# A block's layer norms: means, variances and shifts computed on GpSimd instead of VectorE

## The chip, the core and the metric

The kernel runs on one core of a Trainium2 chip. A core has five engines with queues of their own, each in order: TensorE (PE in the profile, its weight loads are PEld), VectorE (DVE), ScalarE (ACT), GpSimd (POOL) and SyncE (SP, which here only starts DMAs). They wait for one another through semaphores. The metric is the time of one execution in device microseconds (us); lower is better. The profile is one execution on the chip, taken with the hardware profiler; its span, from first to last instruction, is somewhat shorter than the time that the runs give.

## The reference, cut to what matters

`x` has 2048 rows of 512 bfloat16 values. Three layer norms, a windowed attention (32 heads, 8 keys each, two rows apart) and an MLP that mixes the rows:

```
def _layernorm(x, axis=-1, eps=1e-05):
    m = jnp.mean(x, axis=axis, keepdims=True)
    v = jnp.var(x, axis=axis, keepdims=True)
    return (x - m) / jnp.sqrt(v + eps)
...
    h = _layernorm(x, axis=-1) * (1 + ca) + sa          # first norm
    x = x + ga * _A_ref(h, A_wqkv, A_wo)                # attention
    h = _layernorm(x, axis=-1) * (1 + cb) + sb          # second norm
    x = x + gb * _B_ref(h, B_w1, B_b1, B_w2, B_b2)      # MLP over rows
    return x
...
    def _B_ref(x, w1, b1, w2, b2):
        h = _layernorm(x, axis=-1)                      # third norm
        u = _gelu(jnp.einsum('bsd,sf->bdf', h, w1) + b1)
        y = jnp.einsum('bdf,fs->bds', u, w2) + b2
        return y.transpose(0, 2, 1)
```

The six modulation rows (`sa` to `gb`) come from a small matrix product of `silu(c)`.

## The kernel before, in words

The 2048 rows are 16 tiles of 128 rows, in five chunks of 2, 4, 4, 4 and 2 tiles. A chunk goes through: statistics of the first norm (`ln1s`), reciprocal standard deviation (`rstd1`), normalized tiles (`n1`), their transposes (`tr` on TensorE with evictions `hT`, or DMA transposes `xt` in the last three chunks), the projections (`qkv`, evicted by `ev`), products of queries with shifted keys on VectorE (`qk`, 128x4096 elements for a chunk of four tiles), their reduction on TensorE (`red`), maximum, exponential and reciprocal (`max`, `sub`, `exp`, `esum`, `rcp`, `smB`), products of weights with shifted values on VectorE (`pv`), reduction on TensorE (`pvacc`, evicted by `oev`), the output projection (`wo`, evicted by `x1` with the sum of each row), the sum of squares (`ln2q`), the second norm (`rstd2`, `n2`, then `aff`, which multiplies and adds the modulation rows), the statistics of the third norm (`ln3s`) and its result (`rstd3`, `h3`). The MLP's first product (`mlp1`) sums over rows, so it takes one tile of `h3` after another; partial sums are parked in SBUF (`park`) and added later (`inj`, `padd`). After GELU the second product (`mlp2`) and the output (`fin`, `st_out`) follow.

The order of all this is written out by hand: `ORDER` is one list of names, and each engine issues its own in just that order. So an instruction that waits holds back everything behind it on its engine, whatever is ready. `add` records an operation with engine and dependencies; a helper issues them all, so the profile has one source line (L133), and its groups are told apart by their tiles. The tiles to know: `st` (statistics of BN_STATS, 6 values a row), `mv` (mean and variance), `lv` (logarithm), `rs` (reciprocal standard deviation), `nb` (shift, minus mean times `rs`), `sums` (sum and sum of squares), `big` (the attention products), `lsb` (softmax weights), `h` (normalized tiles), `junk` (the unused output of squaring).

The layer norms before:

- `ln_stats`: on VectorE, BN_STATS and an aggregation to `mv`, tile by tile. For tiles 10 to 13 of the first norm ScalarE sums and squares instead, and VectorE forms the variance (`ln1v`).
- The second norm takes sum and square from ScalarE, except tiles 14 and 15; VectorE forms the variance of a group of tiles in two instructions (`ln2m`).
- `ln_rstd`: ScalarE takes a logarithm and an exponential for a group (the chunk in the first norm; 2, 2, 4 or 1 tiles in the others). VectorE multiplies out the shift (`nb`), unless the whole group is normalized on VectorE.
- `ln_norm`: one instruction per tile, on ScalarE, GpSimd or VectorE as the letters A, P and D in `NE` say.

There are 25 such groups: 5 of the first norm, 10 of the second and 10 of the third. `NBIG` gives four buffers for the attention products; `psS` are six PSUM tiles, which the evictions free.

Of the kernel before, what the change touches and what calls it, by code (L numbers as in the profile page):

```python
# [13 lines left out]
P = 128  # L14
# [168 lines left out]
consts ld_x_1_2 act_table ld_x0 ld_x_1_4 ld_c ld_x_2_8 ld_x1 ident ld_x_2_6 ld_wmod1 ln1s3 halo0 ld_wqkv1 cps  # L183
ln1s2 warm2 ld_wqkv0 silu_exp ld_wmod0 ln1s0 ln1s4 ln1s1 ln1s5 rstd1_0 ld_x_4_14 nb1_0 ln1s9 rstd1_1 n1_0 n1_1
silu_dve nb1_1 ld_wqkv2 ln1s8 fill:2:70 tr0_0 n1_2 n1_4 modcols1 ln1s7 hT0_3:a n1_5 n1_3 ld_x_3_10 hT0_2:d a1col
hT0_0:a fill:4:16 tr1_2 wsc1_2:d ld_b1 hT0_1:a wsc1_3:d wsc1_0:a tr1_0 wsc1_1:d ln1s6 hT1_2:a ld_wmod2 qkv0_10
ld_x_3_12 wsc0_0:d rstd1_2 wsc0_1:d qkv0_12 wsc0_2:d hT1_1:a nb1_2 n1_8 n1_9 wsc0_3:d modcols0 hT1_0:d ld_wmod3
hT1_3:a qkv0_00 sab ev0_12:d n1_6 ld_wmod4 qvb0 ln1s14 ld_wo1 qkv0_02 qvb_cp0 ln1s15 ev0_00:a wsc2_2 qvb1
wsc2_0:d qkv1_00 wsc2_3 ev0_10:a ev0_02:d ln1s10 wsc2_1:d qkv1_10 qvb_cp1 qk0_0 ev1_10:a qkv0_22 qk0_1 n1_7
qkv0_20 ln1s13 qk0_2 qkv1_02 xt6 red0_0 ev1_00:a qk0_3 red0_1 red0_2 ev0_22:a ld_wmod5 qkv1_22 qk1_0 ev0_20:a  # L190
qkv1_12 ev1_02:a vd0_1 red0_3 ev1_12:a mask qkv1_11 vd0_0 ln1s11 max0 xt8 qk1_2 qkv1_01 ev1_11:a sub0 qkv1_03
ev1_01:a xt9 exp0 qkv1_13 qk1_1 ev1_03:a xt7 esum0 ev1_13:a qkv1_20 rcp0 vd0_2 ln1s12 qkv1_21 smB0 qk1_3 a2_0_3
modcol2 rstd1_4 qkv1_23 a2_0_0 ev1_22:a a2_0_2 halo_v1:a red1_0 ev1_20:a a2_0_1 red1_1 ln1v10 ln1v12 ln1v11
ln1v13 nb1_4 red1_2 rstd1_3 n1_15 ld_wo3 red1_3 nb1_3 ld_wo2 mcols0 n1_11 n1_10 qkv2_00 max1 ev1_21:a n1_14 xt10
qkv2_02 ev2_00:a pv0_0 qkv2_10 n1_12 ld_wo0 pv0_1 qkv2_11 vd0_3 ev2_10:a ev2_02:a qkv2_12 qk2_0 n1_13 qkv2_01
xt12 ev2_12:a pvacc0_0 ev2_01:a sub1 qk2_2 xt13 qkv2_03 exp1 qkv2_13 xt11 ev2_11:a ev2_03:a qkv2_22 qk2_1
ev2_13:a esum1 ev1_23:a qkv2_21 rcp1 vd1_2 red2_0 smB1 ev2_21:a ld_b2 red2_1 qk2_3 halo_v2:a a2_1_1 red2_2
pvacc0_1 a2_1_3 qkv3_00 a2_1_2 qkv3_10 a2_1_0 pv0_2 mrowt0 vd1_1 qkv2_20 ev3_10:a pv0_3 ev3_00:a red2_3 mrows0:a
qkv2_23 ev2_20:a st_row0 max2 halo_k3:p ev2_22:a vd1_3 qkv3_11 qk3_0 xt14 qkv3_22 ev3_11:a pvacc0_2 ld_row0
pvacc0_3 sub2:q oev0_2:a vd1_0 pv1_2 qkv3_02:q exp2 qkv3_12 ev3_02:a ev2_23:a qkv3_01 pv1_3 oev0_0:a vd2_2 esum2  # L200
modcol3 xt15 rcp2 ev3_12:a woq_s qkv3_20 ev3_01:a pvacc1_3 smB2 ev3_20:a red3_0 qk3_1 ev3_22:a a2_2_0 pvacc1_2
wo1 a2_2_1 vd2_3 qkv3_13:q x1_1 a2_2_2 pv1_1 vd2_1 wo0 ev3_13:a a2_2_3 qkv4_02 ld_w1_0_512 oev1_2:a mcols1 pv1_0
ld_w1_0_0 oev1_3:a mrowt1 qkv3_03 mrows1:a x1_0 st_row1 qkv4_00 ev3_03:a vd2_0 ln2q1 qk3_2 pvacc1_0 ev4_02:a
red3_1 pvacc1_1 oev1_0:a qkv3_23:q oev1_1:a qk3_3 ev4_00:a wo3:q ln2q0 wo5:q pv2_2 qkv4_22:q x1_5 ev3_23:a wo2:q
ld_row1 ln2q5 ld_w1_0_896 ln2m0 halo_v3:a wo4:q x1_3 pv2_1 x1_2 red3_2 x1_4 red3_3 ln2q3 qkv3_21:q pv2_3 rstd2_0
qkv4_20 ln2q2 ev3_21:a ev4_22:a vd3_3 pvacc2_1 nb2_0 max3 pvacc2_2 n2_0 warm0 ln2q4 vd3_0 n2_1 ln2m2 sub3 pv2_0
pvacc2_3 oev2_2:a exp3 rstd2_2 esum3 oev2_1:a aff0 pvacc2_0 rcp3 oev2_0:a qkv4_10 oev2_3:a ln2m4 nb2_2 smB3
warm3 n2_2 ev4_10:a ln3s0 wo6 a2_3_0 n2_3 ln3s1 a2_3_1 rstd2_4 wo7 x1_6 vd3_1 aff2 rstd3_0 a2_3_2 biascols wo9:q
ev4_20:a a2_3_3 nb2_4 nb3_0 ln3s3 n2_5 n2_4 vd3_2 warm1 ln3s2 h3_1 h3_0 qkv4_12 aff4 rstd3_2 wo8 x1_7 ld_w2_0
nb3_2 ln3s5 h3_3 h3_2 ln2q6 ln3s4 mlp1_0_6_0 ev4_12:a pv3_0 mlp1_0_3_0 x1_9 rstd3_4 mlp1_0_5_0 x1_8 mlp1_0_0_0  # L210
biascols_cp:a ln2q8 nb3_4 pv3_1 halo_v4:a mlp1_0_2_0 h3_4 vd4_1 h3_5 mlp1_0_1_0 ln2q9 pv3_2 ld_w2_1 mlp1_0_2_4
vd4_2 ln2q7 mlp1_0_0_4 vd4_0 mlp1_0_3_4 park0_0:a mlp1_0_1_4 mlp1_0_5_4:q park0_1:a ln2m6 vd4_3 pv3_3 park0_2:a
pvacc3_0 pvacc3_1 oev3_0:a ld_w1_0_1152 pvacc3_2 oev3_1:a mlp1_0_4_0:q rstd2_6 oev3_2:a qk4_2 pvacc3_3 park0_3:a
mlp1_0_7_0 oev3_3:a nb2_6 qk4_1 n2_6 mlp1_0_6_4 mlp1_0_4_4 n2_8 qk4_0 wo12:q ld_w1_0_1408 n2_7 n2_9 qk4_3 wo10:q
park0_4:a aff6 x1_12 red4_0 wo13:q ld_w2_3 park0_5:a ln2q12 red4_1 red4_2 x1_10 red4_3 wo11:q max4 ln2q10 ln3s9
x1_13 sub4:q mlp1_0_8_0:q exp4 ln3s8 ln2q13 mlp1_0_11_0 esum4 ln3s7 rcp4 mlp1_0_12_0 park0_6:a ln3s6 x1_11
mlp1_0_10_0 smB4 rstd3_6 ln2m12 a2_4_2 mlp1_0_9_0 h3_7 rstd2_12 h3_6 a2_4_3 ln2q11 h3_9 mlp1_0_8_4 ln2m13 a2_4_0
nb2_12 ln2m11 n2_12 mlp1_0_7_4 a2_4_1 ln2m10 h3_8 rstd2_10 ld_w2_4 aff12 mlp1_0_9_4 rstd2_13 rstd2_11 nb2_10
ln3s12 mlp1_0_9_8 mlp1_0_7_8 n2_10 mlp1_0_8_8 nb2_13 pv4_0 park0_7:a mlp1_0_12_4 ld_w1_0_1664 park0_8:a
mlp1_0_11_4 nb2_11 pv4_2 n2_13 mlp1_0_10_4 rstd3_12 pv4_1 park0_9:a mlp1_0_12_8 n2_11 mlp1_0_10_8 pv4_3 inj1_4  # L220
mlp1_0_11_8 ld_w1_1_0 park0_10:a pvacc4_2 ld_w1_1_640 park0_11:a pvacc4_0 nb3_12 aff11 pvacc4_1 h3_12 pvacc4_3
mlp1_0_13_0 aff10 oev4_0:a oev4_2:a aff13 mlp1_0_13_4 ln3s10 wo15 ld_w2_5 ln3s13 rstd3_10 mlp1_0_13_8 wo14 x1_15
rstd3_13 park0_12:a inj1_0 nb3_13 ln2s15 mlp1_1_0_6 nb3_10 x1_14 rstd2_15 mlp1_1_4_6 park0_13:a nb2_15 ln2s14
n2_15 inj1_3 inj1_6 ld_w1_1_896 inj1_5 mlp1_1_6_6 rstd2_14 aff15 h3_10 mlp1_1_3_6 ln3s15 mlp1_1_6_10 ln3s11
mlp1_1_0_10 rstd3_15 inj1_1 mlp1_1_1_6 park1_0:a nb3_15 h3_15 n2_14 rstd3_11 aff14 mlp1_1_5_6 h3_13 ln3s14
mlp1_1_5_10 mlp1_1_1_10 inj1_2 ld_w1_2_0 mlp1_1_2_6 h3_11 rstd3_14 park1_1:a h3_14 mlp1_1_4_10 mlp1_1_3_10
mlp1_1_2_10 mlp1_1_9_10 park1_2:a ld_w1_1_1408 park1_3:d mlp1_1_7_10 padd1_9 park1_4:a park1_5:d mlp1_1_8_10
padd1_7 gelu7 mlp1_1_10_10 park1_6:a mlp1_2_2_11 ld_w1_2_640 padd1_10 mlp1_2_2_14 mlp1_2_0_11 padd2_2
mlp1_2_0_14 ld_w2_7 gelu2 mlp1_2_1_11 padd2_0 mlp1_2_1_14 gelu0 mlp1_1_12_10 padd2_1 gelu10 padd1_8 gelu1
# [12 lines left out]
def kernel(  # L242
# [52 lines left out]
    def T(shape, dtype, name):  # L295
        return sb.tile(shape, dtype, name=name)
# [38 lines left out]
    epscol = T([P, 1], F32, "epscol")  # L335
# [17 lines left out]
    for l in range(3):  # L353
        for nm, n in (("st6", 6), ("mv", 2), ("lv", 1), ("rs", 1), ("nb", 1)):
            ln_t[nm, l] = T([P, NST, n], F32, f"{nm}_{l}")
# [14 lines left out]
    def ln_stats(l, st, src, reads, name):  # L370
        st6, mv = ln_t["st6", l], ln_t["mv", l]
        if l == 0 and st in LN1A:
            def fa():
                nc.scalar.activation(junk[:], src, ACT.Identity, scale=1.0 / D, accum_out=mv[:, st, 0:1])
                nc.scalar.activation(junk[:], src, ACT.Square, scale=D ** -0.5, accum_out=st6[:, st, 0:1])
            add("act", 1.36, fa, reads=reads + ["act_table"], writes=[("sq", l, st)], name=name)
            add("dve", 0.15, lambda: nc.vector.scalar_tensor_tensor(
                mv[:, st, 1:2], mv[:, st, 0:1], mv[:, st, 0:1], st6[:, st, 0:1], op0=ALU.mult, op1=ALU.subtract,
                reverse1=True), reads=[("sq", l, st)], writes=[("mv", l, st)], name="ln1v" + name[4:])
            return  # L380

        def fd():
            nc.vector.bn_stats(st6[:, st, :], src)
            nc.vector.bn_aggr(mv[:, st, :], st6[:, st, :])
        return add("dve", 0.86, fd, reads=reads, writes=[("mv", l, st)], name=name)

    def ln_rstd(l, g0, n, name, var=None, vreads=None):
        mv, lv, rs, nb = (ln_t[k, l] for k in ("mv", "lv", "rs", "nb"))
        sl = slice(g0, g0 + n)
        var = mv[:, sl, 1] if var is None else var  # L390

        def fa():
            nc.scalar.activation(lv[:, sl, 0], var, ACT.Ln, bias=epscol[:, 0:1])
            nc.scalar.activation(rs[:, sl, 0], lv[:, sl, 0], ACT.Exp, scale=-0.5)
        reads = [("mv", l, st) for st in range(g0, g0 + n)] if vreads is None else vreads
        add("act", 0.54, fa, reads=reads + ["ident", "act_table"], writes=[("rs", l, g0)], name="rstd" + name)
        if vreads is None and NE[l][g0:g0 + n] == "D" * n:
            return
# [640 lines left out]
```

## Time and profile before

| what | value |
|---|---|
| time, median of 2 runs | 207.16 us (206.71 to 207.61) |
| span of the profiled execution | 204.6 us, 4223 instructions |
| VectorE, products of query and key, 128x4096 | 12 x 2284 ns |
| VectorE, products of weight and value, 128x4096 | 12 x 2286 ns |
| VectorE, BN_STATS | 30 x 677 ns |
| VectorE, aggregation of one tile | 30 x 182 ns |
| VectorE, shifts | 21, 145 to 159 ns each |
| ScalarE, logarithm / exponential of a group | 25 x 291 ns / 25 x 204 ns |
| GpSimd, normalization of one tile | 11, 813 ns (9 of `xx`) and 774 ns (2 of `h`) on average |
| granted TensorE clock | full in all windows but the last |

Busy time in us of each window of 5 us, from answers of the trace:

| window | PE | DVE | ACT | POOL |
|---|---|---|---|---|
| 0 to 5 | 1.91 | 1.32 | 1.46 | 2.32 |
| 10 to 15 | 4.74 | 4.77 | 4.73 | 1.52 |
| 45 to 50 | 5.00 | 5.00 | 2.04 | 0.53 |
| 75 to 80 | 4.26 | 4.90 | 4.97 | 0.77 |
| 90 to 95 | 4.32 | 4.91 | 4.69 | 0.77 |
| 110 to 115 | 4.49 | 4.83 | 4.00 | 0.00 |
| 140 to 145 | 5.00 | 2.11 | 2.11 | 0.00 |

Busy shares say how long an engine had an instruction under way. A row of the timeline reads: start, duration, engine, line, operation, output and inputs, sizes, count, and in brackets the idle time of the engine before it with what ended it. "x2" is two instructions merged, with their joint duration. A row of the view of waits names who waited, for whom, the sum, how often, and the longest. Neighbouring instructions of one engine overlap by some hundredths of a microsecond in the records.

### The profile page before, as it was taken

How to read it: one execution, taken by the hardware profiler on the slowest of the kernel's cores; microseconds unless marked ns; L12 is line 12 of the kernel's file. 1: busy time of each engine (PE TensorE's matmuls, PEld its weight loads, DVE VectorE, ACT ScalarE, POOL GpSimd, SP SyncE). 2: the span in 40 equal slices, each digit the busy share in tenths (PEclk: the TensorE clock that was granted, in tenths of full speed). 3: DMA queues.
4: the chain of work that ended last, by engine and by line, in shares of the span. 5: the costliest groups of instructions: out<-in, count | busy, mean ns of one | idle time of the engine just before them, and what ended most of it. 6: DMA issues, size and time to landing. Idle time of an engine off the chain costs nothing.

```text
span 204.6 us, 4223 instructions
## 1 busy us (share of the span) xinstructions
PE 194.7 (95%) x1655; PEld 103.5 (51%) x1655; DVE 163.3 (80%) x260; ACT 120.6 (59%) x283; POOL 13.0 (6%) x36
## 2 busy tenths in 40 slices
PE   3999999999999997989899999999999999999994
PEld 3988554454455553554344445444444444444453
DVE  2899999999999999999999999975473204369365
ACT  2398998994666899989898876683762000000000
POOL 4122001100000001240000000100000000000000
PEclk9999999999999999999999999999999999999999
DMA  5999494646958976194975179946990930121121
GB/s 141 330 380 348 117 239 107 161 98 201 247 186 267 308 234 251 25 272 110 289 200 115 26 157 263 288 131 200 340 304 3 232 88 16 39 77 51 51 82 51
DMA packets 55111, 35.93 MB, mean 176 GB/s; under 512 B 24628, under 2 KB 52404, under 8 KB 55092
## 3 DMA queue, kind: packets, MB, share of 16 engines
q1 hardware_dynamic: 55084, 35.67, 61.4%
q8 instruction: 13, 0.21, 0.4%
q14 instruction: 6, 0.05, 0.1%
q10 hardware_dynamic: 8, 0.00, 0.0%
HBM read 22.55 MB, written 2.10 MB: 121 GB/s over the span
## 4 chain that ended last, share of the span: by engine, by line
PE 65%; DVE 20%; issue 5%; DMA 5%; SPq 3%; ACT 2%; DVEq 0%
PE psS L133 62%; DVE big L133 9%; DVE h L133 3%; PE psL L133 3%; SPq L133 3%; DVE st L133 3%; DMA wst<-in_B_w_dram 2%; DMA xx<-in_A_x_dram 2%; ACT h L133 1%; DVE mv L133 1%; DVE m L133 1%; DVE lsb L133 1%; DVE ls L133 0%; DVE nb L133 0%; DVE woq L133 0%
## 5 line engine op out<-in xcount | busy, mean ns | idle before, releaser
L133 PE MATMUL psS<-h,wst 128*128 128x512 bf16 (+1 forms) x254 | 50.7, 379 | 1.2 <-POOL h L133 0.7
L133 PE MATMUL psS<-hT,w_qkv 128*128 128x512 bf16 (+3 forms) x312 | 46.2, 339 | 0.3 <-ACT w_qkv L133 0.3
L133 PEld LDWEIGHTS <-wst 128*128 128x128 bf16 (+1 forms) x356 | 28.7, 98 | 32.2 <-issue 3.2
L133 PEld LDWEIGHTS <-w_qkv 128*128 128x128 bf16 (+1 forms) x354 | 29.5, 111 | 21.3 <-issue 3.2
L133 DVE TENSOR_TENSOR big<-a2sb,vD 128x4096 bf16<-128x4096 bf16 (+1 forms) x20 | 36.9, 1876 | 0.0
L133 DVE TENSOR_TENSOR big<-q_sb,k_f 128x4096 bf16<-128x4096 bf16 (+1 forms) x20 | 36.3, 1857 | 0.0
L133 DVE SCALAR_TENSOR_TENSOR h<-psS,bcol,rows_bc 128x512 f32<-128x512 f32 (+2 forms) x18 | 12.4, 690 | 24.4 <-PE psS L133 24.2
L133 PE MATMUL psS<-gT,big 128*128 128x512 bf16 x112 | 24.8, 379 | 0.0
L133 PEld LDWEIGHTS <-big 128*128 128x128 bf16 x144 | 12.0, 97 | 13.2
L133 PEld LDWEIGHTS <-ident 128*128 128x128 bf16 (+1 forms) x203 | 13.9, 111 | 5.9 <-issue 2.8
L133 PE MATMUL psS<-woq,o_sb 128*32 128x512 bf16 (+1 forms) x172 | 16.6, 380 | 0.0
L133 ACT ACTIVATE h<-xx,nb,rs 128x512 bf16<-128x512 bf16 x19 | 15.0, 807 | 0.8 <-DVE nb L133 0.7
L133 DVE TENSOR_TENSOR psS<-psS,gT 128x512 f32<-128x512 f32 x14 | 9.3, 696 | 7.0 <-PE psS L133 7.0
L133 ACT ACTIVATE junk<-xx 128x512 bf16<-128x512 bf16 x22 | 13.8, 626 | 0.2
L133 POOL TENSOR_SCALAR h<-xx,rs,nb 128x512 bf16<-128x512 bf16 x9 | 7.3, 813 | 101.3 <-DVE nb L133 84.0
L133 ACT ACTIVATE lv<-mv,epscol 128x1 f32<-128x1 f32 (+2 forms) x25 | 7.3, 291 | 9.3 <-DVE mv L133 8.4
L133 DVE BATCH_NORM_STATS2 st<-xx 128x6 f32<-128x512 bf16 x14 | 9.5, 678 | 4.0 <-DMA xx<-in_A_x_dram 4.0
L133 ACT ACTIVATE gT<-psS,bcol 128x512 bf16<-128x512 f32 x14 | 8.7, 688 | 6.4 <-DVE psS L133 6.4
L133 PEld LDWEIGHTS <-group 128*32 128x32 bf16 x288 | 6.8, 96 | 10.2 <-issue 4.8
L133 DVE TENSOR_TENSOR h<-h,rows_bc 128x512 bf16<-128x512 bf16 (+2 forms) x20 | 11.5, 581 | 0.5
L133 DVE TENSOR_TENSOR h<-h,xx 128x512 bf16<-128x512 f32 (+2 forms) x18 | 11.4, 633 | 0.6
L133 ACT ACTIVATE gT<-psS 128x512 bf16<-128x512 f32 x19 | 10.8, 587 | 1.6 <-PE psS L133 1.5
(94 smaller groups left out, 220.4 us busy)
## 6 DMA issues: line engine op xcount, KB each, us to landing
vD<-v_sb SPq DMA_DIRECT2D x12, 524.5 KB, 3.8
big<-in_B_w_dram SPq DMA_DIRECT2D x4, 896.0 KB, 8.2
vD<-v_sb SPq DMA_DIRECT2D x8, 268.5 KB, 3.0
wst<-in_B_w_dram SPq DMA_DIRECT2D x3, 640.0 KB, 5.3
out_dram<-h SPq DMA_DIRECT2D x15, 128.0 KB, 1.8
xx<-in_A_x_dram SPq DMA_DIRECT2D x7, 256.0 KB, 6.1
wst<-in_B_w_dram SPq DMA_DIRECT2D x2, 800.0 KB, 4.8
gT<-in_w_mod_dram SPq DMA_DIRECT2D x3, 512.0 KB, 6.1
```

The lines of the kernel that those rows point to most:

```text
L133: r = fn(*a, **k)
```

## The change

What VectorE and ScalarE deliver stays: BN_STATS, sums and squares. All that follows on one to eight values a row moves to GpSimd, for the whole group at once. `lnm` is a new operation of GpSimd: for statistics of BN_STATS six instructions (half-row means subtracted, both halves added, the difference squared, the sum of the variances scaled with the epsilon added, the two added, the mean scaled into the shift), for sums four. ScalarE's logarithm reads its result (with a factor of 0.25 for BN_STATS), and the shift `nb` is one more instruction of GpSimd after the exponential. Aggregations, `ln1v` and `ln2m` are gone. All normalizations now read `rs` and `nb`. A memset (`epscol`) goes too, since the epsilon is now an immediate. In `ORDER`, each `lnm` stands immediately ahead of its `rstd`, and four `nb` are new (for groups that had none); the rest is as it was.

```diff
     def ln_stats(l, st, src, reads, name):
...
-        def fd():
-            nc.vector.bn_stats(st6[:, st, :], src)
-            nc.vector.bn_aggr(mv[:, st, :], st6[:, st, :])
-        return add("dve", 0.86, fd, reads=reads, writes=[("mv", l, st)], name=name)
+                nc.scalar.activation(junk[:], src, ACT.Identity, scale=1.0 / D, accum_out=sums[:, st, 0:1])
+                nc.scalar.activation(junk[:], src, ACT.Square, scale=D ** -0.5, accum_out=sums[:, st, 1:2])
+            return add("act", 1.46, fa, reads=reads + ["act_table"], writes=[("st", l, st), ("sums", st)], name=name)
+        return add("dve", 0.66, lambda: nc.vector.bn_stats(st6[:, st, :], src), reads=reads, writes=[("st", l, st)],
+                   name=name)
+
+    def ln_rstd(l, g0, n, name, kind):
+        st6, sm, mv, rs, nb = (ln_t[k, l] for k in ("st6", "sm", "mv", "rs", "nb"))
         sl = slice(g0, g0 + n)
-        var = mv[:, sl, 1] if var is None else var
+        g = nc.gpsimd
+
+        def f():
+            if kind == "bn":
+                g.tensor_tensor(mv[:, sl, 0], st6[:, sl, 1], st6[:, sl, 4], op=ALU.subtract)
+                g.tensor_tensor(sm[:, sl, :], st6[:, sl, 1:3], st6[:, sl, 4:6], op=ALU.add)
+                g.tensor_tensor(mv[:, sl, 0], mv[:, sl, 0], mv[:, sl, 0], op=ALU.mult)
+                g.tensor_scalar(mv[:, sl, 1], sm[:, sl, 1], 4.0 / D, 4.0 * EPS, op0=ALU.mult, op1=ALU.add)
+                first, neg = sm[:, sl, 0], -0.5
+            else:
+                neg = -1.0 if l == 0 else -1.0 / D
+                first = sums[:, sl, 0]
+                g.tensor_tensor(mv[:, sl, 0], first, first, op=ALU.mult)
+                g.tensor_scalar(mv[:, sl, 0], mv[:, sl, 0], -neg * neg, EPS, op0=ALU.mult, op1=ALU.add)
+            second = mv[:, sl, 1] if kind == "bn" else sums[:, sl, 1]
+            g.tensor_tensor(mv[:, sl, 0], mv[:, sl, 0], second, op=ALU.add)
+            g.tensor_scalar(nb[:, sl, 0], first, neg, 0.0, op0=ALU.mult, op1=ALU.add)
 
         def fa():
-            nc.scalar.activation(lv[:, sl, 0], var, ACT.Ln, bias=epscol[:, 0:1])
-            nc.scalar.activation(rs[:, sl, 0], lv[:, sl, 0], ACT.Exp, scale=-0.5)
...
-        add("act", 0.54, fa, reads=reads + ["ident", "act_table"], writes=[("rs", l, g0)], name="rstd" + name)
-        if vreads is None and NE[l][g0:g0 + n] == "D" * n:
-            return
-        mean, k = (mv[:, sl, 0], -1.0) if vreads is None else (sums[:, sl, 0], -1.0 / D)
-        add("dve", 0.15, lambda: nc.vector.scalar_tensor_tensor(nb[:, sl, 0], mean, k, rs[:, sl, 0], op0=ALU.mult,
-                                                               op1=ALU.mult),
-            reads=[("rs", l, g0)] + reads, writes=[("nb", l, g0)], name="nb" + name)
+            nc.scalar.activation(mv[:, sl, 1], mv[:, sl, 0], ACT.Ln, scale=0.25 if kind == "bn" else 1.0)
+            nc.scalar.activation(rs[:, sl, 0], mv[:, sl, 1], ACT.Exp, scale=-0.5)
...
+        add("pool", 0.8, f, reads=keys, writes=[("mv", l, g0)], name="lnm" + name)
+        add("act", 0.53, fa, reads=[("mv", l, g0), "act_table"], writes=[("rs0", l, g0)], name="rstd" + name)
+        add("pool", 0.1, lambda: g.tensor_tensor(nb[:, sl, 0], nb[:, sl, 0], rs[:, sl, 0], op=ALU.mult),
+            reads=[("rs0", l, g0)], writes=[("rs", l, g0)], name="nb" + name)
...
     def build_chunk(ch):
...
-                def f(g0=g0, gn=gn, mv=mv):
-                    gs = slice(g0, g0 + gn)
-                    nc.vector.scalar_tensor_tensor(mv[:, gs, 0], sums[:, gs, 0], -1.0 / D ** 2, sums[:, gs, 0],
-                                                   op0=ALU.mult, op1=ALU.mult)
-                    nc.vector.tensor_tensor(mv[:, gs, 1], mv[:, gs, 0], sums[:, gs, 1], op=ALU.add)
...
+            ln_rstd(1, g0, gn, f"2_{g0}", "bn" if g0 in LN2D else "sums")
```

In `ORDER`, the start as an example (before, after):

```diff
-ln1s2 warm2 ld_wqkv0 silu_exp ld_wmod0 ln1s0 ln1s4 ln1s1 ln1s5 rstd1_0 ld_x_4_14 nb1_0 ln1s9 rstd1_1 n1_0 n1_1
+warm2 ld_wqkv0 silu_exp ld_wmod0 ln1s0 ln1s4 ln1s1 ln1s5 lnm1_0 rstd1_0 ld_x_4_14 nb1_0 ln1s9 lnm1_1 rstd1_1 n1_0 n1_1
```

## The prediction

> **What bounds the kernel now.** I read the page's busy shares first, then the view of who waits for whom on TensorE, then the timeline of the start, then GpSimd's and VectorE's instructions side by side.
>
> ```profile
> PE 194.7 (95%) x1655; PEld 103.5 (51%) x1655; DVE 163.3 (80%) x260; ACT 120.6 (59%) x283; POOL 13.0 (6%) x36
> ```
>
> TensorE is busy 95% of the span of 204.6 us. VectorE's 80% is an average: by windows of 5 us it is busy 4.6 to 5.0 of 5 from 10 to 135 us, and less after. GpSimd looks free, but a free engine is not yet a quick one.
>
> ```profile
> PE psS L133 <- POOL epscol L133: 3.1, 1, 3.1
> PE psS L133 <- DVE big L133: 1.0, 2, 0.7
> PE psL L133 <- DVE m L133: 0.7, 1, 0.7
> PE psS L133 <- POOL h L133: 0.7, 1, 0.7
> PE psS L133 <- ACT lsb L133: 0.6, 1, 0.6
> PE psS L133 <- ACT gT L133: 0.5, 1, 0.5
> PE psS L133 <- ACT w_qkv L133: 0.3, 1, 0.3
> ```
>
> Without the first row (the start) TensorE waits 3.8 us in all, nearly all of it between 79 and 113 us, in the stretch (58 to 112 us) where the chain of waits runs over VectorE. From 112.8 us on the chain is TensorE alone, for 88.75 us. A lighter VectorE can return at most those 3.8 us; whatever makes TensorE wait longer is added whole. The start is a chain through statistics:
>
> ```profile
> 8.34 0.29 ACT L133 ACTIVATE lv<-mv,epscol 128x2 f32<-128x2 f32 x1 [4.87 <-DVE mv L133]
> 9.07 0.30 ACT L133 ACTIVATE lv<-mv,epscol 128x4 f32<-128x4 f32 x1 [0.20 <-DVE nb L133]
> 9.51 0.80 ACT L133 ACTIVATE h<-xx,nb,rs 128x512 bf16<-128x512 bf16 x1
> ```
>
> ScalarE waits for the variances, and its two logarithm-exponential pairs stand ahead of the first normalization, whose result TensorE transposes. Last, the rows on which the forecast rests:
>
> ```profile
> 1.00 0.50 POOL L133 TENSOR_SCALAR_AFFINE_SELECT group<-group 128x32 bf16<-128x32 bf16 x2
> 35.26 1.52 POOL L133 TENSOR_SCALAR h<-xx,rs,nb 128x512 bf16<-128x512 bf16 x2 [17.31 <-DVE mcols L133]
> 36.28 1.57 DVE L133 TENSOR_TENSOR big<-a2sb,vD 128x2048 bf16<-128x2048 bf16 x1
> 45.52 0.68 DVE L133 TENSOR_TENSOR lsb<-lsb,rb 128x1024 bf16<-128x1024 bf16 x1
> 45.76 0.53 POOL L133 COPY k_f<-k_f 128x64 bf16<-128x64 bf16 x1 [8.98 <-DVE big L133]
> 46.12 2.32 DVE L133 TENSOR_TENSOR big<-q_sb,k_f 128x4096 bf16<-128x4096 bf16 x1
> 83.77 0.68 DVE L133 TENSOR_TENSOR lsb<-lsb,rb 128x1024 bf16<-128x1024 bf16 x1
> 83.95 1.15 POOL L133 TENSOR_SCALAR h<-xx,rs,nb 128x512 bf16<-128x512 bf16 x1 [4.48 <-DVE nb L133]
> ```
>
> GpSimd's normalization takes 0.77 us beside VectorE's BN_STATS or a reduce from PSUM, but 1.15 when it begins inside a product of two SBUF tensors: it seems to wait for the product's end at about 84.35. The copy of 64 elements takes 0.53 and ends 0.17 after the next product begins. The other way, the product at 36.28 takes 1.57 instead of 1.21, as a GpSimd instruction runs until 36.78. My reading: a GpSimd instruction that meets such a product waits for its end, then takes its turn; after the tiny copy the next product lasts 2.32 instead of 2.28, so VectorE loses only 0.04.
>
> **The change part by part.** VectorE loses 71 instructions: 30 aggregations (0.18 us each; by start-to-start 0.12), 21 shifts (0.15; 0.07), 16 of the eight two-step variances (0.27 to 0.37 a pair, as 73.59 to 73.96), 4 at 33.79 (0.60 together): 30 x 0.12 + 21 x 0.07 + 8 x 0.35 + 0.6 = 8.5 us. ScalarE's count is unchanged. GpSimd gains 157 (16 groups of 7 from BN_STATS, 9 of 5 from sums) and loses one memset. DMAs and TensorE's order stay.
>
> The price of one tiny GpSimd step that depends on the last: no such row exists. From below 0.10 (memset of 128x1) plus 0.07 gap, 0.17; from above 0.21 plus 0.08 (the AFFINE_SELECT pair), 0.29. I take 0.23, the middle. The Trainium skill (GPSIMD Engine Reference, Engine selection) speaks against the move: two-input elementwise work is given as about twice as slow as on VectorE; an estimate from it, twice the 0.15 us shift, is 0.30 a step, which would put the start's term at its upper end; no row here shows it.
>
> *Start.* Statistics of tile 1 end at 8.02; TensorE's first real work hangs on them. Now 0.1 (wake-up, as 8.24 to 8.34), five steps 1.15, 0.1, logarithm and exponential 0.52 end at 9.89. GpSimd's queue holds the first group's shift ahead of the second group, so another 0.1 + 0.23 + 1.15 + 0.1 until the second logarithm, and 0.44 (9.07 to 9.51) until the first normalization: 11.91 instead of 9.51, +2.4 (1.7 to 3.1). Behind that waiting logarithm stand the normalizations and transposed evictions, and TensorE at 13.61. The third group (tiles 6 to 9) takes 1.08 from statistics (13.84) to VectorE's normalization (14.92); now 2.3, with a weight scaling queued behind it that TensorE needs at 15.78: +1.1 (0.6 to 1.6). GpSimd's two weight scalings (16.59) stand behind the third group's shift and come some 2.3 later, no more than TensorE itself by then. VectorE's saved steps there return 0.3. Term **+3.2** (2.0 to 4.7).
>
> *20 to 58 us.* VectorE gains the 0.7 of 33.79 to 34.50: **-0.5** (-0.8 to 0). The logarithm at 34.42 comes some 0.7 later; what covers it is ScalarE's slack (2.04 of 5 us busy at 45 to 50). Without that cover, 0.7.
>
> *73 to 92 us.* Group 0's squares can be formed early; its last step slips in between products near 75.8, and ScalarE reaches the logarithm at 75.98 anyway: nothing, and up to 2.2 if that gap is missed. Group 2's scale and add meet the product at 79.9 and the affine ones: logarithm at 82.4 instead of 81.26, with the softmax's reciprocal and three evictions queued behind. The third norms of groups 0 and 2 each have five steps among affine products of 0.69: logarithm of group 2 at about 91.8 instead of 89.17, its normalized tiles at 93.8 instead of 91.4. TensorE already waits there for one of them (the 0.7 row). **+2.4** (1.0 to 4.0).
>
> *92 to 102 us.* Third norm of group 4. Four products of 2.2 us follow each other on VectorE, now from 92.9. Its dependent steps fit only at their ends, at 95.1, 97.3 and 99.5 if the unchained ones share a turn; exponential at 100.1, shift at 101.7, two normalizations of ScalarE (1.50 at 94.84) until 103.5 instead of 96.3. TensorE's other work, 22 matmuls of 0.215 after 91.5, is used up at 96.25: 7.2 late, 2.4 already counted, 4.8 left; 2.0 if steps share more turns, 6.0 if fewer, since VectorE soon lacks buffers and stops. I take **+4.0**.
>
> *100 to 115 us.* Second norms of tiles 6 to 9 between products of 1.13, third ones beside BN_STATS, where only latency counts (1.7 instead of 0.5) and TensorE wants the tiles at about 114.5: **+1.5** (0.5 to 3.0).
>
> *115 to 137 us.* ScalarE waits six times for VectorE's statistics (3.6 us in all); tiles 15 and 14 have two norms in series, each 1.2 longer, and the last normalization (135.85) is needed at about 136.3: **+2.5** (1.0 to 4.0). Later nothing changes.
>
> VectorE's own loss: in 70 to 113 us GpSimd gains 48 instructions; at 0.04, 1.9 us, against some 4 saved there, so it is in no term. The Trainium skill (SBUF — State Buffer, SBUF: two separate sides) says that the first holds the shared ports for its whole instruction and the other fully blocks; at 0.2 us each this would be 9.6, and the sum some 5 higher; the 2.32 row speaks against that for tiny ones, the 1.57 row for it with long ones.
>
> Sum 3.2 - 0.5 + 2.4 + 4.0 + 1.5 + 2.5 = 13.1 (ends 5.7 and 21.7). The runs' median of 207.16 lies 2.6 above the profiled span; 204.6 + 13.1 + 2.6 = **220 us**; ends 213 and 229.
>
> **Rivals.** *Latency alone*: GpSimd's steps find gaps and the products hold up nothing. For it: 12 of GpSimd's 13 long instructions last 0.68 to 0.77 us; against: the 0.53 and 1.15 rows, the only ones begun inside a product. Start 3.2, -0.5, one latency of 1.1 in each of the four later stretches: +7.1, 214 us.
> *VectorE freed*: a step costs little more than the 0.035 by which memsets follow each other. It decides where five steps take about 0.06 each and so replace the 0.32 from statistics to logarithm: the start is unchanged and TensorE's 3.8 us come back, 203.4; at 0.17 a step the start takes 2.0 of them back, 205.4. Against: the AFFINE_SELECT pair, and the step's wait for its predecessor.
> *Every instruction loses a product of its own*, unchained ones too, and the latency is at its upper end: 229 to 236.
> That the edit does nothing is excluded by the two engines' instruction lists.
>
> **How the numbers follow.** Forecast 0.60, latency alone 0.20, VectorE freed 0.11, every instruction 0.09. The range 211 to 229 leaves out the last two. Two per cent, about what a measurement here can tell, is 203.0 to 211.3: faster 0.02 (the freed case with a shorter start as well), within 0.13 (the rest of it, 0.09, and a fifth of latency alone, 0.04), slower 0.85.
>
> **What would show it.** Right: ScalarE's first normalization near 12 us instead of 9.51; TensorE's longest new wait near 97 to 103 us for ScalarE's normalized tiles; GpSimd rows of 2 us for 2 to 8 elements, ending at the ends of VectorE's products; VectorE idle where it had none. Wrong: GpSimd rows of 0.1 to 0.2 throughout (latency alone, or freed), TensorE's waits unchanged in the start, or VectorE's products lengthened by more than 0.1 each.

## The result, and the profile after

The changed kernel takes 224.38 us, the median of 2 runs (224.28 to 224.48), against 207.16 before: a ratio of 1.0825, with a 95% interval of 1.0764 to 1.0887. The profiled execution's span grew from 204.6 to 222.7 us.

The busy shares and the clock row of the page come first:

```profile
PE 198.0 (89%) x1635; PEld 104.1 (47%) x1655; DVE 157.2 (71%) x189; ACT 117.7 (53%) x283; POOL 74.5 (33%) x192
PEclk9999999999999999965999998899999999999999
```

VectorE did get lighter: 71 instructions and 6.1 us less (157.2 for 163.3), where the prediction had counted 8.5. GpSimd went from 13.0 to 74.5 us, far more than 157 tiny instructions cost when nothing holds them. And the granted clock, which was full nearly throughout before, has two dips, at slices 18 and 19 and at 25 and 26 (of 5.6 us each). The first five rows of nine in the view of TensorE's waits (who, for whom, sum, times, longest):

```profile
PE psS L133 <- POOL h L133: 10.0, 2, 8.6
PE psS L133 <- POOL ident L133: 3.1, 1, 3.1
PE psS L133 <- ACT gT L133: 2.8, 3, 2.2
PE psS L133 <- ACT h L133: 1.3, 1, 1.3
PE psS L133 <- DVE w_qkv L133: 1.0, 1, 1.0
```

Without the row of the start (3.1 both times) TensorE waits 17.1 us over all rows, where it waited 3.8: 13.3 more. Half of the 17.1 is one wait of 8.6 us for one tile that GpSimd normalizes. The timelines of VectorE, GpSimd and TensorE show it, first in the changed kernel:

```profile
94.41 9.29 DVE L133 TENSOR_TENSOR big<-a2sb,vD 128x4096 bf16<-128x4096 bf16 x4
94.59 6.98 POOL L133 TENSOR_SCALAR h<-h,rs,nb 128x512 bf16<-128x512 bf16 x1
101.54 2.22 POOL L133 TENSOR_TENSOR mv<-st 128x2 f32<-128x2 f32 x1
101.62 9.73 PE L133 MATMUL psS<-h,wst 128*128 128x512 bf16 x38 [8.62 <-POOL h L133]
```

The same place in the kernel before:

```profile
90.69 0.77 POOL L133 TENSOR_SCALAR h<-h,rs,nb 128x512 bf16<-128x512 bf16 x1 [1.62 <-DVE nb L133]
91.52 7.18 PE L133 MATMUL psS<-h,wst 128*128 128x512 bf16 x38 [0.68 <-POOL h L133]
92.22 2.29 DVE L133 TENSOR_TENSOR big<-a2sb,vD 128x4096 bf16<-128x4096 bf16 x1
94.42 0.15 DVE L133 SCALAR_TENSOR_TENSOR nb<-mv,rs 128x2 f32<-128x2 f32 x1
94.50 4.48 DVE L133 TENSOR_TENSOR big<-a2sb,vD 128x4096 bf16<-128x4096 bf16 x2
98.90 0.15 DVE L133 SCALAR_TENSOR_TENSOR mv<-sums 128x4 f32<-128x4 f32 x1
```

There VectorE's shift of tiles 4 and 5 and its variance of tiles 6 to 9 part the four products; the change moves both to GpSimd.

VectorE's four products of weight and value (`pv3`) begin at 94.41. The third norm's normalization of tile 2 begins 0.18 later and lasts 6.98 us instead of 0.77. It passes neither at the end of the first product nor at that of the second; the third ends at about 101.1. In the kernel before the same instruction ran at 90.69, ahead of the row. Behind it in GpSimd's queue stand the steps for tiles 4 and 5, whose logarithm makes ScalarE wait 7.44 us, until 104.53.

The 38 matmuls behind the wait take 9.73 us; before, the same 38 took 7.18. The windows say why (window, busy time of PE, PEld, DVE, ACT, POOL, then the clock, the DMA share and GB/s):

```profile
95.00:100.00 5.00, 0.00 (x0) 0.00 (x0) 5.00 (x3) 2.09 (x6) 5.00 (x1) 0.66 0.07 12
100.00:105.00 5.00, 3.38 (x9) 1.17 (x9) 3.71 (x2) 0.44 (x3) 4.57 (x7) 0.50 0.01 3
105.00:110.00 5.00, 5.00 (x20) 2.12 (x19) 0.00 (x0) 4.20 (x13) 0.96 (x5) 0.82 0.43 104
```

The clock fell to half while TensorE was idle, and stayed there for the first matmuls. Later, from 131 to 136 us, the same thing happens on a smaller scale, with products of 1.14 us:

```profile
131.48 1.18 POOL L133 TENSOR_TENSOR mv<-st 128x1 f32<-128x1 f32 x1
132.61 1.18 POOL L133 TENSOR_TENSOR sm<-st 128x2 f32<-128x2 f32 x1
...
134.90 1.17 POOL L133 TENSOR_SCALAR mv<-sm 128x1 f32<-128x1 f32 x1
```

Four steps on one or two values a row, of the third norm of tile 12, take one product each. ScalarE's logarithm behind them is late, an eviction (`gT`) behind it too, and TensorE waits 2.19 us, until 137.35.

One product is not the most that a tiny step can lose. GpSimd in the changed kernel, then the same step in the kernel of the experiment that keeps TensorE busy (below):

```profile
21.55 6.84 POOL L133 TENSOR_SCALAR nb<-sm 128x2 f32<-128x2 f32 x1
```

```profile
20.90 1.23 POOL L133 TENSOR_SCALAR nb<-sm 128x2 f32<-128x2 f32 x1
```

In both, five products of query and key follow one another on VectorE, and the step begins 0.02 to 0.03 us behind the first. Once it gets in at the first end; once it loses four ends and gets in only at the fifth, where VectorE goes on with a reduction that reads PSUM. It lasts 6.84 us in five of the profiled kernels and 1.23 in three. TensorE loses nothing by it here (+2.1 us at 20 us, +2.2 at 92).

Where the 18.1 us of span come from, by comparing TensorE's position at the same matmul in the two timelines: +2.1 at 20 us; still +2.2 just before the long wait; +12.6 when the 38 matmuls are done (7.9 more waiting, 2.5 more matmul time); +11.4 at 124 us, mainly since two waits of before (0.73 and 0.52) shrink to 0.25 in all; and +18.1 at the end (waits of 0.54, 2.19, 1.33 and 0.33, and 2.3 more, most of it in the windows around the second clock dip, at 0.75 and 0.90).

### The profile page after: what moved, and what is told of

Its sections match the earlier page's. It is cut to its first block, busy times and chain, and to the rows that moved or that the text cites. A ratio compares the mean times of both kernels' runs of the same rounds, so it can differ in the third digit from the quotient of the medians.

```text
span 222.7 us, 4305 instructions
## 1 busy us (share of the span) xinstructions
PE 198.0 (89%) x1635; PEld 104.1 (47%) x1655; DVE 157.2 (71%) x189; ACT 117.7 (53%) x283; POOL 74.5 (33%) x192
## 4 chain that ended last, share of the span: by engine, by line
PE 56%; POOL 17%; DVE 11%; ACT 8%; issue 4%; DMA 2%; SPq 1%; POOLq 0%; DVEq 0%; ACTq 0%
PE psS L133 53%; POOL mv L133 9%; DVE big L133 5%; POOL h L133 5%; PE psL L133 3%; POOL nb L133 2%; DMA xx<-in_A_x_dram 2%; DVE st L133 2%; DVE h L133 2%; ACT mv L133 2%; POOL sm L133 2%; ACT rs L133 1%; ACT xx L133 1%; ACT h L133 1%; SPq L133 1%
## 5 line engine op out<-in xcount | busy, mean ns | idle before, releaser
L133 PE MATMUL psS<-h,wst 128*128 128x512 bf16 (+1 forms) x249 | 54.5, 397 | 11.3 <-POOL h L133 8.6
L133 PEld LDWEIGHTS <-wst 128*128 128x128 bf16 (+1 forms) x356 | 29.6, 101 | 45.6 <-issue 19.0
L133 ACT ACTIVATE mv<-mv 128x1 f32<-128x1 f32 (+2 forms) x25 | 5.1, 203 | 32.1 <-POOL mv L133 32.1
L133 PEld LDWEIGHTS <-ident 128*128 128x128 bf16 (+1 forms) x203 | 13.3, 109 | 6.1 <-issue 3.0
L133 POOL TENSOR_TENSOR mv<-st 128x1 f32<-128x1 f32 (+2 forms) x16 | 6.7, 420 | 23.4 <-DVE st L133 23.4
L133 POOL TENSOR_TENSOR nb<-nb,rs 128x1 f32<-128x1 f32 (+2 forms) x25 | 7.5, 305 | 20.7 <-ACT rs L133 17.9
L133 PE MATMUL psS<-big,group 128*32 128x512 bf16 (+1 forms) x160 | 10.0, 355 | 2.3 <-ACT gT L133 2.2
```

The lines of the kernel that those rows point to most:

```text
L133: r = fn(*a, **k)
```

## The experiments

The question was which of three things makes up the loss: the latency of the steps, the one starved normalization (tile 2's, held over several products), or the steps of tiles 4 and 5 that the prediction named. In all diffs the rest is as in the changed kernel unless it says otherwise; "the kernel before" was run beside each on the same chip (206.75 to 206.94 us median). A ratio is given with its 95% interval where there were several runs; it is an estimate from all of them, not the quotient of the two medians.

**One norm at a time.** Each kernel is the kernel before with the groups of one norm handed to the changed kernel's function.

```diff
-        ln_rstd(0, t0, nt, f"1_{ch}")
+        if (0, t0) in ON_POOL:
+            ln_rstd_pool(0, t0, nt, f"1_{ch}", "sums" if t0 in LN1A else "bn")
+        else:
+            ln_rstd(0, t0, nt, f"1_{ch}")
```

> Only the first layer norm's groups (five of the 25) get their means, variances and shifts on GpSimd; the second and third norms stay on VectorE. Theory A (the prediction's steps): the start costs +3.2 and 20 to 58 us return 0.5, so about +2.7 against the kernel before. Theory B (the changed kernel's trace, where TensorE stands 2.17 later at 91 us): +2.2, and nothing after. Both: TensorE's wait at the start is longer, the rest as before, granted clock near 0.998. Rival (a GpSimd step that loses products also stretches VectorE's work): +4 or more.

> Only the second layer norm's ten groups get their means, variances and shifts on GpSimd. Theory A (the prediction's steps): about 1.2 of the 2.4 at 73 to 92 us, 0.8 of the 1.5 at 100 to 115 us and 1.2 of the 2.5 at 115 to 137 us: +3.2. Theory B (starvation): the cost comes only where one GpSimd instruction is held over several products and TensorE's spare work runs out, and the changed kernel's trace shows that for the third norm alone: +1 or less up to 131 us, then up to +1.5.

> Only the third layer norm's ten groups get their means, variances and shifts on GpSimd. Theory A (the prediction's steps): 1.2 at 73 to 92 us, 4.0 at 92 to 102 us, 0.7 and 1.3 behind it: +7, with TensorE waiting for ScalarE's normalized tiles of group 4. Theory B (starvation): GpSimd's 512-wide normalization of tile 2 begins just inside the row of 2.27 us products and lasts about 7 us; TensorE waits 8 to 9 us for it, its clock falls to 0.5 to 0.7 for some 8 us after, another 2 us are lost to the four steps of 1.17 us at 131 to 136 us: +12 to +15. Rival (phase): without the first norm's 2.2 us shift the normalization gets in ahead of the products, as in the kernel before, and TensorE waits 3 us or less there: +3 to +6.

Measured: 210.56, 207.49 and 219.88 us (one run each), so +3.8, +0.7 and +13.1 against 206.75. Together that is 17.6, and the whole change costs 17.2 to 17.6: as far as single runs can tell, the three parts add up.

The first norm alone costs more than either figure expected. Its trace shows part of this to be chance: the DMA brought tile 1 later, its statistics ended at 8.6 instead of 8.02 us. From GpSimd's first step to ScalarE's first normalization it takes 3.03 us, exactly as in the changed kernel. TensorE waits 3.2 us for the first of these tiles, and the granted clock is 0.78 and 0.88 in the windows from 10 to 20 us, where the changed kernel has it full.

The second norm costs nothing until 131 us. TensorE even stands 0.85 us earlier at 112 us, 0.4 of that from an earlier start; then it waits 1.59 us, until 132.74, for a tile that ScalarE normalizes behind the logarithm of tile 14's second norm.

The third norm carries three quarters of the loss. The rival (phase) falls: without the first norm's delay the normalization of tile 2 still starts 0.18 us inside the first product, at 93.21, and again lasts 6.98 us; TensorE waits 8.7 us for it.

**The starved normalization moved away.**

```diff
-    NE=('PAPAAPAADAAPAAPD', 'PAPAAPAAAADAAADP', 'APPAAADDDDADAADA'),
+    NE=('PAPAAPAADAAPAAPD', 'PAPAAPAAAADAAADP', 'APAAAADDDDADAADA'),
```

> The changed kernel, with one instruction moved: the third norm's normalization of tile 2 is formed by ScalarE instead of GpSimd. Theory B (starvation of this one instruction): TensorE's wait of 8.6 us shrinks to 3.5 or less, the clock dip after it is smaller or gone, and the time falls by 4 to 9 us, to 215 to 220. Theory A (the prediction: the steps of group 4's third norm, one to a product, are late by themselves): the wait moves to ScalarE's normalized tiles of group 4, and the time falls by 3 us at most. If starvation were only a symptom of late statistics, nothing changes within 1 us.

Measured: 224.39 us, 1.0823 times the kernel before (1.0777 to 1.0869). Nothing was gained; Theory B as I had put it falls. TensorE now waits 3.15 us for ScalarE's tile 2, then 2.56 more for an eviction that stands behind ScalarE's logarithm, and at a lower clock its 38 matmuls take 5.99 + 5.85 us. The reason is what the prediction had described. GpSimd's timeline:

```profile
95.39 2.17 POOL L133 TENSOR_TENSOR mv<-st 128x2 f32<-128x2 f32 x1
97.52 2.25 POOL L133 TENSOR_TENSOR sm<-st 128x4 f32<-128x4 f32 x1
99.72 2.24 POOL L133 TENSOR_TENSOR mv<-mv 128x2 f32<-128x2 f32 x1
101.93 2.23 POOL L133 TENSOR_SCALAR mv<-sm 128x2 f32<-128x2 f32 x1
```

With tile 2 out of the queue, the steps of tiles 4 and 5 come forward into the row of products, and each leaves at the end of one. The logarithm comes at 104.47; in the changed kernel it came at 104.53.

**Tiles 4 and 5 moved back, alone and with tile 2.** The third norm of these two tiles is on VectorE again, all else on GpSimd; in the second kernel tile 2 is on ScalarE as well.

```diff
-ON_POOL = [..., (2, 0), (2, 1), (2, 2), (2, 3), (2, 4), (2, 5), (2, 6), ...]
+ON_POOL = [..., (2, 0), (2, 1), (2, 2), (2, 3), (2, 6), ...]
```

> The changed kernel, with the third norm of tiles 4 and 5 alone back on VectorE (two aggregations, one shift, logarithm with the epsilon column); tile 2 is normalized by GpSimd as in the changed kernel. Theory B (one starved instruction, the normalization of tile 2): no change within 1.5 us, TensorE's longest wait stays near 8 us for GpSimd's h. Theory C (the queue of GpSimd over the row of VectorE products decides, whoever stands in it, and either of the two is enough): likewise no change within 1.5 us. Theory A (the five dependent steps of this group alone, as the prediction put it): 4 us less, 220.

> The changed kernel, with both: third norm of tiles 4 and 5 on VectorE and tile 2 normalized by ScalarE, so that GpSimd holds nothing that TensorE needs while the four 2.27 us products run. Theory C (either is enough, so only both together help): 9 to 13 us less, 212 to 215, and the granted clock near 0.99 throughout. Theory A: 4 us less. If late statistics by themselves are the cause: 2 us less or nothing.

Measured: 217.17 us for the first (one run) and 218.36 for the second (ratio to the kernel before 1.0575, 1.0525 to 1.0626). One group returned is worth 7.2 us, more than any theory had for it, and moving tile 2 besides gains nothing: TensorE then waits 3.17 us for ScalarE's tile 2. The second expectation was missed because in the first kernel the normalization of tile 2 is not starved any more: two aggregations stand again between the statistics and the row, so the first product begins at 94.75, and the normalization at 94.40 is in before it. TensorE's wait there is 2.41 us. A head start of 0.35 us decided it.

With both moved, the span is still 11.7 us above the kernel before. By TensorE's position, 2.1 of that are there at 20 us, 2.5 come in the stretch up to the end of the 38 matmuls, and 7.6 behind the matmul that starts at 112.83 in the kernel before, where waits of 0.55, 2.18, 0.35 and 2.21 us stand. In the runs of one norm each, the third has 4.0 us behind that point, the second 1.8 and the first nothing; no run takes this last stretch apart further, so its cause is read from rows and not tested.

**That head start taken away again.** To the kernel with 217.17 us, one more GpSimd instruction ahead of tile 2's:

```diff
+        def on_pool():
+            if l == 2 and st == 2:
+                nc.gpsimd.tensor_scalar(late[:], src, args[0], args[1], op0=args[2], op1=args[3])
+            nc.gpsimd.tensor_scalar(dst, src, args[0], args[1], op0=args[2], op1=args[3])
```

> The kernel with the third norm of tiles 4 and 5 on VectorE (215.4 us of span), with one more GpSimd instruction of 0.77 us (a copy of the normalization of tile 2, result not used) ahead of the normalization of tile 2. In that kernel the normalization began at 94.40, 0.35 us before the first product; now it begins about 95.1, inside it. Starvation: it lasts 4 to 7 us instead of 0.77, TensorE waits 6 to 8 us for it instead of 2.41, and the time rises by 4 to 7 us. If group 4's steps alone were the cause: TensorE waits 0.6 to 0.8 us longer and the time rises by less than 1.5 us.

GpSimd and VectorE in it:

```profile
94.97 2.55 DVE L134 TENSOR_TENSOR big<-a2sb,vD 128x4096 bf16<-128x4096 bf16 x1
95.38 2.79 POOL L134 TENSOR_SCALAR h<-h,rs,nb 128x512 bf16<-128x512 bf16 x1
97.57 0.60 DVE L134 SCALAR_TENSOR_TENSOR nb<-mv,rs 128x2 f32<-128x2 f32 x1
```

220.29 us (one run), 3.1 more; TensorE waits 5.16 us there, and its 38 matmuls take 9.43. So the starvation of tile 2 is real and costs by itself, but less than expected, since it lasts one product only. The third line shows why: here VectorE forms the shift of tiles 4 and 5 between the first product and the second, and at that end GpSimd gets in (95.38 + 2.79 = 98.17, the end of the shift, which takes 0.60 us instead of 0.15). In the changed kernel this shift has gone to GpSimd too, as has the variance ahead of the fourth product, and the four products follow one another without a gap.

**One group alone.** The kernel before, with only the third norm of tiles 4 and 5 on GpSimd.

```diff
+ON_POOL = [(2, 4), (2, 5)]
```

> The kernel before, with one group of the 25 moved: the third norm of tiles 4 and 5 gets its means, variances and shift on GpSimd. The two tiny VectorE steps of that group (its aggregations ahead of the row of four 2.27 us products, its shift between the first two) are gone. Theory (each GpSimd step waits for the end of one product, independent ones too, as the two engines alone showed): four steps end at about 94.4, 96.6, 98.9 and 101.1, the fifth just behind, its logarithm near 101.5 instead of 94.1 or so, TensorE waits some 6 to 8 us behind it (for ScalarE's eviction queued behind the logarithm, then for the normalized tiles), and the time rises by 5 to 9 us: as much as this group gave back (7.2 us) when it alone was returned to VectorE. If instead starvation of the normalization of tile 2 was the whole cost: here that runs before the products, as in the kernel before, and the time rises by 1.5 us at most.

Measured: 214.19 us, 1.0342 times the kernel before (1.0292 to 1.0392), +7.3. GpSimd's timeline, then TensorE's:

```profile
91.85 2.16 POOL L134 TENSOR_TENSOR mv<-st 128x2 f32<-128x2 f32 x1 [0.39 <-DVE st L134]
93.97 2.25 POOL L134 TENSOR_TENSOR sm<-st 128x4 f32<-128x4 f32 x1
96.17 2.24 POOL L134 TENSOR_TENSOR mv<-mv 128x2 f32<-128x2 f32 x1
98.38 0.19 POOL L134 TENSOR_SCALAR mv<-sm 128x2 f32<-128x2 f32 x1
```

```profile
91.51 3.18 PE L134 MATMUL psS<-h,wst 128*128 128x512 bf16 x14 [0.69 <-POOL h L134]
99.94 6.00 PE L134 MATMUL psS<-h,wst 128*128 128x512 bf16 x24 [5.25 <-ACT xx L134]
```

Seven instructions on two to four values a row, 1 group of 25, cost 7.3 us. The first three leave at the ends of three products; the row breaks there, since the fourth product stands behind a step that waits for ScalarE, and ScalarE stands at the logarithm. TensorE waits 5.25 us for an eviction (`xx`) behind that logarithm, and then its 24 matmuls take 6.00 us, 2.0 more than before: 5.25 + 2.0 is the 7.2 by which TensorE is late behind them (105.94 instead of 98.70). Tile 2 was normalized in time here, at 90.69.

**Gaps in the row.** The changed kernel, with a BN_STATS behind each product.

```diff
                     nc.vector.tensor_tensor(pv(), a2sb.unsqueeze(2).to_broadcast([P, 2, 4, C]),
                                             _ap(vD_r[s_v.i][:, 2:3], [[-2, 2], [C + PAD, 4], [1, C]]), op=ALU.mult)
+                    if ch == 3:
+                        nc.vector.bn_stats(gap6[:], a2sb[:, 0, :])
```

> The changed kernel, with one more BN_STATS of 512 elements (0.6 us on VectorE, result not used) behind each of the four 2.27 us products; nothing else is changed. If GpSimd's steps are held by products in a row and pass beside BN_STATS (as the run with the two engines alone shows): the normalization of tile 2 lasts about 3 us instead of 6.98, the steps of tiles 4 and 5 pass two or three to a gap, TensorE's wait of 8.6 us falls to 4 to 5, some of it comes back as a wait for tiles 4 and 5, and the time falls by 2 to 5 us although VectorE has 2.4 us more to do. If the loss is one of late statistics or of GpSimd's speed: 0 to 2.4 us slower.

Measured: 222.14 us (1.0753 times the kernel before, 1.0711 to 1.0795), 2.2 less than the changed kernel, with 2.4 us more work on VectorE. The normalization of tile 2 lasts 2.74 us, TensorE's wait for it falls to 4.38, and waits of 1.29, 0.71 and 0.33 for ScalarE come back behind it.

**TensorE kept busy in the long wait.**

```diff
-    WARM=4,
+    WARM=20,
```

with the 16 new blocks (`warm4` to `warm19`) ahead of `mlp1_0_6_0` in `ORDER`.

> The changed kernel, with 16 more blocks of nine 128x128 transposes by the identity (results not used) ahead of TensorE's first matmuls of the token MLP, so that TensorE works during the 8.6 us in which it waited for GpSimd's tile 2. If the falling clock is a cost of that idle time: the granted clock stays near 1 from 95 to 110 us, the 38 matmuls behind take 7.2 to 8.3 us instead of 9.73, and the time falls by 1.5 to 2.5 us. If the clock fell for another reason, or the lost time is hidden: no change within 0.7 us.

Measured: 223.54 us (one run), 0.84 less, short of the 1.5 to 2.5 expected. The clock stays full from 95 to 110, and all 40 matmuls of the stretch take 7.82 us, where 38 took 9.73; so the lost clock is a consequence of the idle time, and worth some 2.3 us there. But little of it reaches the end: 0.76 of the 0.84 is an earlier start, and a new dip (0.75 from 145 to 150 us, behind a wait of 2.48) takes back the rest.

**The two engines alone.**

> Leaves the whole computation out (copies x to the output) and measures the two engines by themselves: VectorE runs nothing, 8 products of two 128x4096 bf16 tensors in SBUF, 6 such products with a BN_STATS after each, 12 BN_STATS, 8 one-tensor scalings of 128x4096, or 12 adds of a PSUM tile; beside it GpSimd runs 5 dependent tiny steps, 5 independent ones, or one 128x512 scaling and a tiny copy. The prediction's reading (a GpSimd instruction that meets a product waits for its end, then takes its turn): each dependent step ends one product (about 2.3 us) after the last, independent ones share a turn, the 128x512 scaling waits for one product only, and VectorE's products are held up by less than 0.1 by a tiny step. Starvation (a GpSimd instruction can lose several ends of products): some steps last two products or more, and the 128x512 scaling lasts until the row of products ends. Both: 0.19 a step, 0.27 from one dependent step to the next, beside nothing, BN_STATS and PSUM adds; with a BN_STATS after each product every step gets in at the first one. Open: whether one-tensor scalings hold GpSimd up as well.

```diff
+    def product(name, n):
+        for i in range(n):
+            nc.vector.tensor_tensor(Z[i % 2][:], X[:], Y[:], op=ALU.mult)
...
+    def chain(name, go):
+        a = T([P, 4], F32, "a" + name)
+        nc.gpsimd.tensor_tensor(a[:], go, go, op=ALU.add)
+        for i in range(2):
+            nc.gpsimd.tensor_scalar(a[:], a[:], 0.5, 0.1, op0=ALU.mult, op1=ALU.add)
+            nc.gpsimd.tensor_tensor(a[:], a[:], a[:], op=ALU.mult)
```

From its timeline; the tiles are named after what VectorE does and what GpSimd does:

```profile
12.62 0.20 POOL L38 TENSOR_SCALAR a_nothing_chain<-a_nothing_chain 128x4 f32<-128x4 f32 x1
12.90 0.20 POOL L38 TENSOR_TENSOR a_nothing_chain<-a_nothing_chain 128x4 f32<-128x4 f32 x1
...
18.63 2.11 POOL L38 TENSOR_SCALAR a_product_chain<-a_product_chain 128x4 f32<-128x4 f32 x1
20.82 2.12 POOL L38 TENSOR_TENSOR a_product_chain<-a_product_chain 128x4 f32<-128x4 f32 x1
...
51.58 17.69 DVE L38 TENSOR_TENSOR Z<-X,Y 128x4096 bf16<-128x4096 bf16 x8
51.74 10.98 POOL L38 TENSOR_TENSOR l_product_loose<-go_product_loose 128x4 f32<-128x4 f32 x5 [6.71 <-DVE go_product_loose L38]
...
87.15 6.97 POOL L38 TENSOR_SCALAR w_product_wide<-src,go_product_wide 128x512 bf16<-128x512 bf16 x1 [6.74 <-DVE go_product_wide L38]
...
106.16 17.24 POOL L38 TENSOR_SCALAR w_product_wide<-src,late_product_wide 128x512 bf16<-128x512 bf16 x1 [9.86 <-ACT late_product_wide L38]
...
197.33 1.17 POOL L38 TENSOR_SCALAR a_single_chain<-a_single_chain 128x4 f32<-128x4 f32 x1
```

Beside nothing, BN_STATS or PSUM adds, a dependent step follows the last by 0.28 us and an independent one by 0.15. Beside a row of products each tiny step takes one product of 2.2 us here, and the five independent ones do too (10.98 us for 5): they share no turn. The one-tile normalization loses the ends of two products and gets in at the third (6.97, where it took 6.98 in the changed kernel); where it began a little later in the row it lost them all and ran when the row was over (17.24). VectorE loses nothing to the tiny steps: eight products take 17.7 us beside each kind, and 18.11 where the normalization got in. That every tiny step gets in at the first end is so in this run, but not always in the kernels: one took 6.84 us there (above), and with the first norm alone a copy of 64 elements a row lost three ends (5.03 us, where it takes 0.53 to 0.56 in the kernel before and the changed one). With a BN_STATS behind each product, every tiny step and the normalization get in at the first one. And the open question has an answer: scalings of one 128x4096 tensor hold GpSimd as well, one step to each (1.17).

**What is worth keeping.** The second norm's groups on GpSimd, without the last two tiles, the rest on VectorE.

```diff
+ON_POOL = [(1, st) for st in range(14)]
```

> Only the second norm's groups of tiles 0 to 13 on GpSimd; tiles 14 and 15 (for which TensorE waited 1.59 us in the run with the whole second norm) and the first and third norms stay on VectorE. By that run TensorE stood 0.85 us earlier than in the kernel before until the last of these waits, 0.4 of it from an earlier start: 0.3 to 0.6 us faster than the kernel before, at most 1; not more, since TensorE waits only 3.8 us in all there. Rival (any step on GpSimd costs): the same or up to 1 us slower.

Measured over 12 runs: 206.52 us against 206.94 for 17 runs of the kernel before, a ratio of 0.9982 (0.9960 to 1.0003). That fits the 0.3 to 0.6 expected, but the interval reaches past 1: a gain is not shown.

## Why the prediction was right, step by step

*The number.* 220 us was forecast, with a range of 211 to 229; 224.4 was measured. The sum of 13.1 us was a sum of waits, and TensorE's waits grew by 13.3. That these two agree is luck: stage by stage the terms were 3.2, 1.9, 4.0, 1.5 and 2.5, the measured changes 2.1, 0, 7.9, -1.2 and 4.4. What the sum lacked is the clock: TensorE's matmuls run slower after long waits, 2.5 us behind the wait of 8.6 and most of 2.3 later on. Against it, the runs lie 1.7 above the span, not the 2.6 taken over.

*Start, +3.2 (2.0 to 4.7).* Measured +2.1. The normalization was forecast for 11.91 from statistics at 8.02, so 3.9 later; it comes 3.1 later (10.77 from about 7.65). The step was taken at 0.23; dependent ones turned out at 0.28, but three of five do not depend on the one before and follow at 0.15, so five take 0.9 instead of 1.15. The estimate of 0.30 a step drawn from the Trainium skill (GPSIMD Engine Reference, Engine selection) is close to the dependent step and twice the other. The weight scaling behind the third group is late as forecast: TensorE waits 1.02 us for `w_qkv`, forecast +1.1.

*20 to 92 us, -0.5 and +2.4.* Measured nothing: +2.1 at 20 us and +2.2 at 92. The steps of the third norm of tiles 0 to 3 found turns among the affine products of 0.69 at 0.2 to 0.66 each, and the lighter VectorE took 0.4 off the wait for `m` and all of one for `big`. This term was too high; the run with the second norm alone shows the same. The prediction's reading that a GpSimd instruction waits for the end of the one product that it meets did not hold there for one step (6.84 us at 21.55), which cost nothing.

*92 to 102 us, +4.0.* This is where the loss is, and its mechanism, steps held by the row of four products, is shown: by the run with that group alone (+7.3), by its return (-7.2, though that freed tile 2 as well), and by its steps' rows. But in the changed kernel another instruction stood first in the same queue. The prediction took a 512-wide normalization for 0.77 us, or 1.15 when it meets a product; it lasted 6.98, and TensorE's longest wait was for GpSimd's tile 2, not for ScalarE's tiles 4 and 5. Each of the two holds TensorE by itself, which is why removing tile 2 alone gained nothing. For tiles 4 and 5 alone the wait was sized well: 5.25 us in the run with that group alone, where the prediction had worked out 4.8 before it took 4.0. What made the term short was the instruction ahead of them and the clock, which the prediction did not count (2.0 us in that run, 2.5 in the changed kernel): +10.4 stood here. That independent steps share a turn was wrong too: each has one of its own.

*100 to 115 us, +1.5.* Measured -1.2 between the 38 matmuls and 124 us. After the long wait everything there was early enough, and the waits of before vanished.

*115 to 137 us, +2.5.* Measured 4.4 of waits, 6.7 with the clock. Latency had been counted, 1.2 us for each of two norms in series; the four steps of 1.17 beside the products of tiles 14 and 15 had not. No run tests what they alone cost.

*VectorE's own loss, in no term.* Right: none beside tiny steps. The Trainium skill (SBUF — State Buffer, SBUF: two separate sides) says that whichever of the two starts first holds the shared ports for its whole instruction while the other blocks, and the estimate from it was 9.6 us of loss on VectorE. That GpSimd blocks, the traces confirm in each row above. The other half, VectorE blocked by tiny steps, is below what can be seen here: 17.70 us for eight products with five steps beside them, and 18.11 with one normalization.

*The rivals.* Latency alone (214) is refuted by GpSimd's rows of 2.2 and 7.0 us. VectorE freed (203.4) is what the second norm alone shows up to 131 us: half a microsecond. Every instruction losing a product of its own (229 to 236) is nearly right as to the mechanism where products stand in a row (some lose more than one), but most of the 157 instructions do not meet such a row.

What stays open: at which end of a product a waiting GpSimd instruction gets in. A 512-wide one got in at the second, at the third or only at the end of the row, a tiny one mostly at the first, but one at the fifth. Its size does not decide it, since the same tiny step, begun at the same place within 0.02 us, did both. The traces do not show the arbitration.

## What to carry to other kernels

Before tiny steps are moved to GpSimd, look at what VectorE runs while they are due: beside BN_STATS or adds that read PSUM they cost 0.28 us each, but beside a row of large products from SBUF each one costs at least a whole product, and a chain of five costs the row. Look also at what the move takes out of that row, since VectorE's own small steps between products were the gaps in which GpSimd ran. And where removing one late instruction gains nothing, ask who stands behind it in the same queue, and remove that one alone before dropping the theory.

## What was not expected of the hardware

A GpSimd instruction can be shut out for a whole row of VectorE products: a 512-wide one 6.97 us through three and 17.24 us through eight, a step on two values a row 6.84 us through five. Mostly a tiny one leaves at the end of the first. One-tensor bf16 scalings of 128x4096 on VectorE hold GpSimd as products do (1.17 us for a step of 0.19).

A wait of TensorE costs more than its length. Behind 8.62 us of idle time the granted clock was 0.50 in the next window, and the following matmuls lost 2.5 us. The Trainium skill (TensorE: Matmul & The Clock Gate, Part 1: The HAM clock gate) says that the clock is halved after an idle window of about 3.4 us and released after about as long a busy one; the long wait agrees with that. Shorter waits do not fit it: the windows also show 0.75 around a wait of 2.19 us in the changed kernel and 0.66 around one of 2.20 in the kernel with tiles 4 and 5 returned, while waits of 2.17 and 2.18 us left the clock full in four kernels (tile 2 on ScalarE and tiles 4 and 5 returned among them) and were followed by 0.66 and 0.81 in two others (BN_STATS between the products; tile 2 delayed). The length of the wait alone does not decide it.
